# Joint conversion steps for the weight tiles, a ten-step inverse root and another written order at the start of a fused attention and feed-forward kernel

## The chip, the cores and the metric

One core of a Trainium2 chip runs the whole program. The metric is its device time in microseconds, from the first to the last instruction of an execution. Five engines work side by side, each through its own list of instructions in order: TensorE (PE, matrix products; its weight loads are PEld), VectorE (DVE), ScalarE (ACT), GpSimd (POOL) and SyncE (SP, which here issues the transfers). An instruction that waits for another engine or a transfer holds up everything behind it on its own engine.

## The reference

The program computes attention with a window of 32 and 32 global tokens, and then a gated feed-forward layer on the result:

```python
# 8 batches, 8 heads, 512 local and 32 global tokens, head size 64
out_g = np.matmul(sm(scale * q_g @ k_all.T), v_all)
s_ll = np.where(np.abs(pos[:, None] - pos[None, :]) <= 32, scale * q_l @ k_l.T, -1e9)
out_l = np.matmul(sm(np.concatenate([scale * q_l @ k_g.T, s_ll], -1)), v_all)
x = np.concatenate([out_g, out_l], 2)      # as 4608 tokens of 512
xn = x / np.sqrt(np.mean(x * x, -1) + 1e-6) * rms_g
g, val = xn @ w_gate, xn @ w_val           # 512 to 1536 each
y = (g / (1 + np.exp(-g)) * val) @ w_out   # 1536 to 512
```

The weights come as float64.

## The kernel before

The 4608 tokens are done in chunks. Chunk 0 is one batch of 512 local tokens. The attention of chunk 0 (units 0 to 3, each two heads) comes first, then its inverse root, its turned and scaled rows, and its feed-forward products, among which units 4 to 7 (the next chunk's attention) stand. All instructions of all engines stand in one list, ORDER, whose entries are chunk, step and piece, `0:g2.1` for the second piece of step g2 of chunk 0; each engine issues its own in that order. The steps are defined in JOBS's order, and in this order every tile draws its page of SBUF from the table PAGES (43 pages of 1024 words a partition, 8 wide ones) and its PSUM bank from BANKS. A transfer into a page can be issued only when the last reader of the page's former tile is done.

The letters of steps that the prediction speaks of, k being a number of a unit, a tile or a turn:
- L, V: loads of queries and keys, of values. S, M, E, T, C, A, X, Q, Z: scores (PE), mask (DVE), exponent (ACT), turn (PE), copy (ACT), value products (PE), division (DVE), squares (ACT), sums (DVE) of an attention unit.
- N0.i: the inverse root of chunk 0's mean squares, 13 small steps on DVE. D0: four diagonal 128x128 tiles with the roots (DVE). U0.k: PE turns the rows of x by multiplying with the diagonals, four 128x128 f32 matmuls for each k; H0.k (ACT) and Y0.k (DVE) write the high and low f16 halves.
- W: load of weight tile i, two transfers of 512 KB. Tiles 0 to 11 are the gate and value weights, 12 to 17 the output weights. m: rebias the exponent by a multiply (DVE if i is in MULT_V, else ACT). s: shift left by 3 (DVE). k or l: fetch the three low bits, on ACT ("three") if i is in LOW_A, else on DVE ("low"). g: put the sign in (DVE). q, p, e: squares and their scale (ACT, PE, DVE). a, d: high (ACT) and low (DVE) f16 weights.
- I f.wi: products of feed-forward tile f, six 128x512 f16 matmuls for each. B, b, h: its activation. O, o: output products and their end.

Each of m, k or l and g works on the two raw halves of a tile, one after another, 128x512 each; s, q, a and d work on 128x1024. All instructions go through one helper, so the trace names the one line L2095 for every row; tiles are told apart by kind (`page`, `bank`, `rn` for the root's small numbers, `ss` for the sums, `ws` for a weight scale, `wd` for a spilled tile in DRAM).

Of the kernel before, what the change touches and what calls it, by code (L numbers as in the profile page):

```python
# [2335 lines left out]
```

## Time and profile before

| | |
|---|---|
| median of 3 runs | 891.29 us (890.4 to 891.63) |
| profiled execution, span | 890.5 us |
| PE busy | 864.1 us, 97% |
| PEld busy | 666.4 us, 75% |
| DVE busy | 709.7 us, 80% |
| ACT busy | 557.9 us, 63% |
| POOL busy | 277.8 us, 31% |

A share is the busy time of an engine over the span. The span has very different stages, so the shares are read from the stage that a change touches.

### The profile page before, as it was taken

The numbers are of one execution on the slowest core, as the hardware profiler recorded it, in microseconds if no ns is written. First come the engines' busy times: TensorE is split into PE (matmuls) and PEld (weight loads), VectorE is DVE, ScalarE is ACT, GpSimd is POOL, SyncE is SP. The second block draws the span as 40 slices with busy tenths as digits, with TensorE's granted clock in tenths as the row PEclk, the third lists the DMA queues.
The fourth block names the chain that finished last, engine by engine and source line by source line (L and its number), as shares of the span: only waits on it lengthen the run. The fifth ranks groups of instructions, "written<-read, shape, count | busy, mean of one in ns | idle before, by whom it ended". The sixth has DMA issues, their size and how long they took to land.

```text
span 890.5 us, 28310 instructions
## 1 busy us (share of the span) xinstructions
PE 864.1 (97%) x11646; PEld 666.4 (75%) x11646; DVE 709.7 (80%) x1857; ACT 557.9 (63%) x1362; POOL 277.8 (31%) x255
## 2 busy tenths in 40 slices
PE   5599999999999999999999999999999999999998
PEld 4554455545548885588888888888888888888997
DVE  5999999798686776777886899688886798587576
ACT  6999993657344664557473876568575772545343
POOL 0000000024834475414531255123441344124414
PEclk9699999999999999999999999999999999999999
DMA  9995340488974997984697567968796759747671
GB/s 353 407 392 190 96 142 25 141 277 283 374 253 143 288 304 230 312 266 150 218 376 263 172 224 218 339 234 291 254 366 206 253 152 366 262 140 229 229 255 62
DMA packets 102737, 216.79 MB, mean 243 GB/s; under 512 B 8272, under 2 KB 34640, under 8 KB 102608
## 3 DMA queue, kind: packets, MB, share of 16 engines
q1 hardware_dynamic: 102176, 214.66, 70.9%
q8 instruction: 91, 1.49, 0.7%
q10 hardware_dynamic: 432, 0.33, 0.1%
q14 instruction: 38, 0.31, 0.1%
HBM read 187.96 MB, written 27.00 MB: 241 GB/s over the span
## 4 chain that ended last, share of the span: by engine, by line
PE 85%; DMA 3%; DVE 3%; issue 1%; ACT 1%; SPq 1%; POOL 0%; DVEq 0%; POOLq 0%; ACTq 0%
PE bank L2095 85%; DVE page L2095 3%; DMA wide<-wd 1%; DMA page<-in_vb_dram 1%; DMA page<-in_gv_dram 1%; ACT page L2095 1%; DMA wb<-page 1%; SPq L2095 1%; POOL page L2095 0%; DVE wide L2095 0%; DVE xg L2095 0%; DVE ws L2095 0%; DVE sm L2095 0%; DVE hs L2095 0%; DVE pow L2095 0%
## 5 line engine op out<-in xcount | busy, mean ns | idle before, releaser
L2095 PE MATMUL bank<-page,page 128*128 128x256 f16 (+7 forms) x8406 | 726.8, 277 | 16.4 <-ACT page L2095 8.0
L2095 PEld LDWEIGHTS <-page 128*128 128x128 f16 (+1 forms) x5568 | 515.7, 98 | 159.4 <-issue 7.6
L2095 POOL TENSOR_TENSOR page<-page,page 128x512 f16<-128x512 f32 (+5 forms) x163 | 180.0, 1122 | 286.4 <-ACT page L2095 236.1
L2095 DVE TENSOR_TENSOR page<-bank,page 128x512 f32<-128x512 f32 (+1 forms) x179 | 113.9, 649 | 64.2 <-PE bank L2095 37.5
L2095 ACT COPY page<-bank 128x512 f32<-128x512 f32 (+3 forms) x172 | 86.9, 529 | 111.2 <-PE bank L2095 100.0
L2095 ACT CAST page<-page 128x512 f16<-128x512 f32 (+2 forms) x144 | 109.0, 780 | 73.5 <-DVE page L2095 59.9
L2095 ACT ACTIVATE page<-page,sm 128x128 f32<-128x128 f32 x344 | 126.5, 391 | 26.7 <-DVE sm L2095 21.7
L2095 DVE TENSOR_TENSOR page<-page,page 128x256 f32<-128x256 f32 (+4 forms) x145 | 90.5, 636 | 9.0 <-ACT page L2095 7.0
L2095 POOL TENSOR_TENSOR page<-page,sm 128x512 f32<-128x512 f32 x22 | 25.5, 1167 | 208.9 <-DVE sm L2095 201.0
L2095 ACT ACTIVATE page<-page 128x512 f32<-128x512 f32 (+2 forms) x93 | 77.1, 907 | 9.6 <-DVE page L2095 7.2
L2095 DVE CUSTOM_DVE_ANT_0 page<-bank,page 128x128 f32<-128x128 f32 x248 | 60.3, 283 | 19.9 <-PE bank L2095 18.8
L2095 PEld LDWEIGHTS bank<-page,page 64*32 64x32 f32 (+4 forms) x3072 | 55.2, 113 | 24.5 <-issue 11.0
L2095 PE MATMUL bank<-wide,page 32*64 32x96 f32 (+6 forms) x2074 | 63.4, 266 | 1.3 <-DMA page<-in_vb_dram 1.3
L2095 ACT ACTIVATE page<-page,half_inv 128x512 f32<-128x512 f32 (+1 forms) x68 | 44.7, 686 | 23.9 <-DVE page L2095 19.3
L2095 DVE TENSOR_TENSOR page<-page 128x256 f32<-128x256 f32 (+3 forms) x110 | 57.1, 533 | 1.1 <-PE bank L2095 0.2
L2095 PE MATMUL bank<-page,wide 128*128 128x256 f16 (+4 forms) x500 | 56.9, 269 | 0.8 <-DMA wide<-wd 0.8
L2095 DVE SCALAR_TENSOR_TENSOR page<-page,page 128x512 f32<-128x512 f32 (+1 forms) x68 | 46.8, 702 | 12.7 <-ACT page L2095 12.7
L2095 DVE SCALAR_TENSOR_TENSOR page<-page,c_h,page 128x512 f32<-128x512 f32 (+1 forms) x73 | 51.8, 728 | 0.7
L2095 PEld LDWEIGHTS <-wide 128*128 128x128 f16 x450 | 41.6, 98 | 13.9 <-DMA wide<-wd 1.1
L2095 ACT ACTIVATION_READ_ACCUMULATOR page<-page,sm 128x1 f32 x248 | 46.8, 189 | 0.0
L2095 POOL TENSOR_TENSOR page<-wide,page 128x512 f16<-128x512 f32 (+2 forms) x25 | 27.4, 1105 | 45.4 <-ACT page L2095 43.3
L2095 PEld LDWEIGHTS bank<-wide,page 32*64 32x64 f32 (+2 forms) x1936 | 29.5, 129 | 6.8 <-issue 2.7
(156 smaller groups left out, 662.1 us busy)
## 6 DMA issues: line engine op xcount, KB each, us to landing
page<-wd SPq DMA_DIRECT2D x117, 512.0 KB, 6.9
page<-wb SPq DMA_DIRECT2D x36, 512.0 KB, 7.0
page<-in_w_in_dram SPq DMA_DIRECT2D x24, 512.0 KB, 9.3
page<-wa SPq DMA_DIRECT2D x23, 512.0 KB, 6.4
page<-wd SPq DMA_DIRECT2D x42, 256.0 KB, 5.3
page<-in_qkb_dram SPq DMA_DIRECT2D x23, 448.0 KB, 6.1
wide<-in_gkq_dram SPq DMA_DIRECT2D x16, 576.0 KB, 8.1
page<-in_vw_dram SPq DMA_DIRECT2D x16, 512.0 KB, 9.3
```

What stands on the lines that cost most here:

```text
L2095: return lambda *a, **k: write(self.engine, lambda: call(*a, **k))
```

## The change

1. CHAINS puts some pages side by side in one tile. Where the two raw halves of a weight tile lie on neighbouring pages, in either order, m, k or l and g run as one instruction over 1024 columns. That is so for all 18 tiles.
2. MULT_V and LOW_A change: seven tiles' multiply on DVE instead of six; tiles 3 and 14 have their low bits fetched on DVE, tile 15 on ACT.
3. The inverse root of chunks 0 and 1 takes ten steps: two rounds with other constants instead of three.
4. ORDER is written anew in its first part (636 entries before, 599 now), which is chunk 0 and the head of the next chunk. The 3118 entries behind it are the same.
5. PAGES (1198 entries) and BANKS (438) are new as a whole.

The code, with the tables ORDER, PAGES and BANKS left out:

```diff
@@ -38,85 +38,86 @@
...
-Q1 W3 X2 Q2 W4 W5 e0 Z1 a0 A3 X3 Q3 e1 a1 L7 Z2 Z3 N0.0 N0.1 N0.2 N0.3 N0.4 N0.5 m2 N0.6 N0.7 N0.8
-N0.9 N0.10 N0.11 N0.12 D0 U0.0 U0.1 U0.2 U0.3 k2 m3 k3 d0 s2 m4 s3 H0.0 H0.1 g2 s4 H0.2 H0.3 Y0.0
...
+W3 X2 Q2 W4 W5 e0 Z1 a0 A3 X3 Q3 e1 a1 L7 Z2 Z3 N0.0 N0.1 N0.2 N0.3 N0.4 N0.5 m2 N0.6 N0.7 N0.8 N0.9
+D0 U0.0 U0.1 U0.2 U0.3 k2 m3 k3 d0 s2 m4 s3 H0.0 H0.1 g2 s4 H0.2 H0.3 Y0.0 q2 Y0.1 Y0.2 L4 Y0.3 m5
...
 NPAGE, NWIDE = 43, 8
 
+CHAINS = (
+    (7, 8, 22, 25), (9, 10), (12, 11, 18), (13, 40), (14, 4, 27, 23, 39), (15, 26), (16, 17),
+    (28, 29), (30, 31), (32, 33), (34, 35), (41, 42),
+)
+
 ORDER = """
...
@@ -493,10 +494,19 @@
 
 
 
-    page = [con.tile([P, 1024], F32, tag=f"page{i}", name=f"page{i}") for i in range(NPAGE)]
+    page, link = {}, {}
+    for n, chain in enumerate(CHAINS):
+        whole = con.tile([P, 1024 * len(chain)], F32, tag=f"chain{n}", name=f"chain{n}")
+        for j, i in enumerate(chain):
+            page[i] = whole[:, 1024 * j : 1024 * (j + 1)]
+            if j:
+                link[chain[j - 1], i] = whole[:, 1024 * (j - 1) : 1024 * (j + 1)]
+    for i in range(NPAGE):
+        if i not in page:
+            page[i] = con.tile([P, 1024], F32, tag=f"page{i}", name=f"page{i}")
     wide = [con.tile([P, 1152], F32, tag=f"wide{i}", name=f"wide{i}") for i in range(NWIDE)]
     banks = [psum.tile([P, 512], F32, tag=f"bank{i}", name=f"bank{i}") for i in range(8)]
-    page_at, bank_at, smalls = iter(PAGES.split()), iter(BANKS.split()), [0]
+    page_at, bank_at, smalls, last_at = iter(PAGES.split()), iter(BANKS.split()), [0], [""]
 
     def tile_of(shape, dt, name):
         n = int(np.prod(shape[1:])) * (2 if dt in (F16, BF16) else 4) // 4
...
             return con.tile(shape, dt, tag=tag, name=tag)
-        at = next(page_at)
+        at = last_at[0] = next(page_at)
         if n > 1024:
             t = wide[int(at[1:])][:, :n]
         else:
@@ -575,12 +585,12 @@
             nc.gpsimd.tensor_tensor(dst, a, b, ALU.subtract)
 
 
-    MULT_V = (0, 1, 3, 7, 11, 12)
-    LOW_A = (2, 3, 4, 5, 6, 9, 10, 11, 13, 14, 16)
+    MULT_V = (0, 1, 3, 8, 9, 11, 15)
+    LOW_A = (2, 4, 5, 6, 9, 10, 11, 13, 15, 16)
     def raw_tile(name):
         return tile_of([P, 1024], I32, name)
 
-    job = {}
+    job, same_piece = {}, [False]
 
     def power(ps, n, top, dst):
 
...
@@ -646,15 +656,23 @@
     def convert(i):
 
         src = w_in[i] if i < NF else w_out[i - NF]
-        raws = []
+        raws, last = [], {}
         t = []
 
         def load():
+            pair, at = [], []
             for w in range(2):
-                raw = raw_tile(f"wr{i}{w}")
-                nc.sync.dma_start(raw, src[:, w, :].bitcast(I32))
-                r = raw.rearrange("p (n t) -> p n t", t=2)
-                raws.append((slice(w * 512, (w + 1) * 512), r[:, :, 0], r[:, :, 1], raw))
+                pair.append(raw_tile(f"wr{i}{w}"))
+                at.append(int(last_at[0][:-1]) if last_at[0][:1].isdigit() else -1)
+            turned = (at[1], at[0]) in link
+            for w in range(2):
+                nc.sync.dma_start(pair[w], src[:, 1 - w if turned else w, :].bitcast(I32))
+            both = link.get(tuple(at[::-1] if turned else at))
+            if both is not None:
+                raws.append((slice(0, 1024), both.bitcast(I32)))
+            else:
+                raws.extend((slice(w * 512, (w + 1) * 512), pair[w]) for w in range(2))
+            last[0] = pair[1]
 
         def rebias():
 
@@ -664,7 +682,9 @@
                 else raw_tile(f"w{i}t")
             )
             t32[i] = f32(t[0])
-            for c, _, hi, _ in raws:
+            for c, raw in raws:
+                hi = raw.rearrange("p (n t) -> p n t", t=2)[:, :, 1]
+                same_piece[0] = raw is not raws[0][1]
                 if i in MULT_V:
                     nc.vector.tensor_single_scalar(f32(t[0][:, c]), f32(hi), REBIAS, ALU.mult)
                 else:
@@ -675,14 +695,15 @@
 
         def three():
 
-            for _, _, _, raw in raws:
+            for _, raw in raws:
                 half = raw.bitcast(I16).rearrange("p (n t) -> p n t", t=4)
                 nc.scalar.activation(
                     half[:, :, 2], half[:, :, 1], AF.Copy, bias=-0.5 + 2.0**-14, scale=2.0**-13
                 )
 
         def low():
-            for _, _, _, raw in raws:
+            for _, raw in raws:
+                same_piece[0] = raw is not raws[0][1]
                 half = raw.bitcast(U16).rearrange("p (n t) -> p n t", t=4)
                 nc.vector.tensor_single_scalar(
                     half[:, :, 2], half[:, :, 1], 13, ALU.logical_shift_right
@@ -690,14 +711,16 @@
 
         def sign():
 
-            for c, _, hi, _ in raws:
+            for c, raw in raws:
+                same_piece[0] = raw is not raws[0][1]
+                hi = raw.rearrange("p (n t) -> p n t", t=2)[:, :, 1]
                 nc.vector.scalar_tensor_tensor(
                     t[0][:, c], hi, ends, t[0][:, c], ALU.bitwise_and, ALU.bitwise_or
                 )
 
         def squares():
             if i < NF:
-                sq_in[i] = raws[1][3].bitcast(BF16)[:, :1024]
+                sq_in[i] = last[0].bitcast(BF16)[:, :1024]
                 nc.scalar.activation(sq_in[i], t32[i], AF.Square, accum_out=ssq[:, i : i + 1])
             else:
                 junk = tile_of([P, 1024], BF16, f"wq{i}")
@@ -705,7 +728,7 @@
                     junk, t32[i], AF.Square, accum_out=rowsq[:, i - NF : i - NF + 1]
                 )
 
-        third = ("k", three) if i in LOW_A else ("l", low)
+        third = ("k", three if i in LOW_A else low)
         for n, fn in (("W", load), ("m", rebias), ("s", shift), third, ("g", sign), ("q", squares)):
             job[f"{n}{i}"] = fn
 
...
@@ -1306,13 +1329,26 @@
         steps = [
             lambda: nc.vector.tensor_reduce(z, ch["ss"], axis=AX.X, op=ALU.add),
             lambda: nc.vector.tensor_scalar(a, z, 1.0 / DM, 1.0e-6, ALU.mult, ALU.add),
-        ] + list(root_steps(a, y, z))
+        ] + list(root_short(a, y, z))
         for i, s in enumerate(steps):
             job[f"N{c}.{i}"] = s
         job[f"D{c}"] = factors
         for n, fn in zip("UHY", (turn, high, low)):
             for k in range(NK):
                 job[f"{n}{c}.{k}"] = lambda fn=fn, k=k: fn(k)
+
+    def root_short(a, y, z):
+        yi = y.bitcast(I32)
+        k = 0.375**0.5
+        yield lambda: nc.vector.tensor_scalar(
+            yi, a.bitcast(I32), -0.5, float(0x5F1FFFF9), ALU.mult, ALU.add
+        )
+        for first, second in ((-0.703952253, 0.703952253 * 2.38924456), (-k, 1.875)):
+            yield lambda: nc.vector.tensor_tensor(z, y, y, ALU.mult)
+            yield lambda w=first: nc.vector.scalar_tensor_tensor(z, z, w, a, ALU.mult, ALU.mult)
+            if second == 1.875:
+                yield lambda: nc.vector.scalar_tensor_tensor(z, z, 1.25 / k, z, ALU.add, ALU.mult)
+            yield lambda w=second: nc.vector.scalar_tensor_tensor(y, z, w, y, ALU.add, ALU.mult)
 
     def root_steps(a, y, z):
         yi = y.bitcast(I32)
@@ -2075,8 +2111,9 @@
 
     def write(engine, call):
         c, step, n, on = at_work
+        joined, same_piece[0] = same_piece[0], False
         if on and (on != engine or engine in ("vector", "gpsimd") or c and step[0] in "Rtn"):
-            n += 1
+            n += not (joined and on == engine)
         at_work[2:] = n, engine
         name = f"{c}:{step}.{n}"
         assert name not in plan or name == next(reversed(plan)), name

```

What the tables do to the order is shown at three places. First DVE, at the end of the inverse root and the diagonals of chunk 0 (`rn` holds the root, `ident` times `rn` is a diagonal, `ends` goes with the sign step). Before, with the sums' gathering on top:

```order
L2095 TENSOR_REDUCE rn_1_160<-ss_8_169 128x4
L2095 TENSOR_SCALAR rn_1_160<-rn_1_160 128x4 x3
L2095 TENSOR_TENSOR rn_1_160<-rn_1_160 128x4
L2095 SCALAR_TENSOR_TENSOR rn_1_160<-rn_1_160 128x4 x2
L2095 TENSOR_SCALAR page_71<-page_71 128x1024
L2095 TENSOR_TENSOR rn_1_160<-rn_1_160 128x4
L2095 SCALAR_TENSOR_TENSOR rn_1_160<-rn_1_160 128x4 x2
L2095 TENSOR_TENSOR rn_1_160<-rn_1_160 128x4
L2095 SCALAR_TENSOR_TENSOR rn_1_160<-rn_1_160 128x4 x2
L2095 SCALAR_TENSOR_TENSOR page_71<-page_74,ends,page_71 128x512
L2095 TENSOR_SCALAR page_95<-ident,rn_1_160 128x128 x4
L2095 SCALAR_TENSOR_TENSOR page_82<-page_70,ws_9_170,page_82 128x1024
```

After, from the seventh step of the root on:

```order
L2132 TENSOR_TENSOR rn_1_142<-rn_1_142 128x4
L2132 TENSOR_SCALAR hs<-bank_96,kk 128x1
L2132 SCALAR_TENSOR_TENSOR rn_1_142<-rn_1_142 128x4 x3
L2132 TENSOR_SCALAR page_82<-ident,rn_1_142 128x128 x2
L2132 TENSOR_SCALAR half_inv<-ws_11_154,ginv_e 128x1
L2132 TENSOR_SCALAR page_82<-ident,rn_1_142 128x128
L2132 TENSOR_SCALAR page_76<-page_76 128x1024
L2132 TENSOR_SCALAR page_82<-ident,rn_1_142 128x128
L2132 SCALAR_TENSOR_TENSOR page_76<-chain_63,ends,page_76 128x1024
L2132 SCALAR_TENSOR_TENSOR page_83<-chain_66,ws_9_152,page_83 128x1024
L2132 TENSOR_SCALAR page_77<-page_77 128x1024
```

The shift of tile 2 (128x1024) and its sign (now 128x1024 in one) have moved behind the root, the shift between the third and the fourth diagonal; two small scale steps (`hs`, `half_inv`) stand among the root's end and the diagonals.

Second PE, from the last value products of chunk 0 on (32x64) over the turns with the diagonals (128x128). Before:

```order
L2095 MATMUL bank_119<-page_84,page_76 32x64 x16
L2095 MATMUL bank_119<-page_77,page_76 32x64 x16
L2095 MATMUL bank_115<-page_95,page_80 128x128 x4
L2095 MATMUL bank_116<-page_95,page_87 128x128 x4
L2095 MATMUL bank_117<-page_95,page_87 128x128 x4
L2095 MATMUL bank_114<-page_95,page_80 128x128 x4
L2095 MATMUL bank_121<-page_69,page_95 32x128
L2095 MATMUL bank_120<-page_69,page_95 32x128
```

After, the same place, and then the end of the scale sum of tiles 2 and 3 with what follows it:

```order
L2132 MATMUL bank_101<-page_83,page_76 32x64 x16
L2132 MATMUL bank_96<-page_82,page_79 128x128 x4
L2132 MATMUL bank_98<-page_82,page_79 128x128 x4
L2132 MATMUL bank_101<-chain_67,chain_68 32x128
L2132 MATMUL bank_99<-chain_67,chain_68 32x128
L2132 MATMUL bank_103<-one_120,chain_64 128x1
L2132 MATMUL bank_96<-page_82,page_80 128x128 x4
L2132 MATMUL bank_100<-page_82,page_80 128x128 x4
L2132 LDWEIGHTS chain_65
L2132 MATMUL bank_102<-page_75,chain_65 128x512
```

Two of the four turns have moved behind the scores of unit 4 (32x128) and the scale sum (128x1). The first products (128x512) follow the fourth turn; before, they followed the scale sum.

Third DVE, the conversion of tile 1, the first to be converted. Before, the two halves from their two pages:

```order
L2095 TENSOR_SCALAR page_68<-page_70 128x512
L2095 TENSOR_REDUCE g_149<-gvec 128x1 x2
L2095 TENSOR_SCALAR page_70<-page_70 128x512
L2095 TENSOR_SCALAR page_68<-page_71 128x512
L2095 TENSOR_SCALAR page_68<-page_68 128x1024
L2095 TENSOR_SCALAR page_71<-page_71 128x512
L2095 SCALAR_TENSOR_TENSOR page_68<-page_70,ends,page_68 128x512
L2095 SCALAR_TENSOR_TENSOR page_68<-page_71,ends,page_68 128x512
```

After (ISA is the mask of a score tile and the reading of its minimum):

```order
L2132 TENSOR_SCALAR page_78<-chain_63 128x1024
L2132 TENSOR_SCALAR page_78<-page_78 128x1024
L2132 ISA page_75,sm_4_147<-bank_102,page_75 128x128
L2132 ISA sm_4_147 128x1
L2132 TENSOR_SCALAR chain_63<-chain_63 128x1024
L2132 ISA page_76,sm_4_147<-bank_103,page_75 128x128
L2132 ISA sm_4_147 128x1
L2132 SCALAR_TENSOR_TENSOR page_78<-chain_63,ends,page_78 128x1024
```

The halves have become one instruction each, and mask steps of the attention stand between them.

## Rows read from the trace of the kernel before

**Rows 1.** Windows: stretch, its us, busy us (x instructions) PE PEld DVE ACT POOL, PEclk, DMA share, GB/s

```profile
5.62:21.30 15.68, 13.17 (x344) 9.23 (x344) 11.65 (x80) 14.14 (x60) 0.00 (x0) 0.89 1.02 400
21.30:32.62 11.32, 8.86 (x227) 7.35 (x226) 10.21 (x33) 11.29 (x32) 0.00 (x0) 0.70 1.02 408
32.62:36.54 3.92, 0.00 (x1) 0.00 (x0) 3.59 (x12) 3.92 (x6) 0.00 (x0) 1.00 1.04 404
36.54:40.06 3.52, 0.00 (x0) 0.03 (x1) 3.31 (x15) 3.52 (x6) 0.00 (x0) 0.50 1.02 408
40.06:43.37 3.31, 3.31 (x15) 3.31 (x16) 3.31 (x5) 3.29 (x4) 0.00 (x0) 0.50 1.02 404
43.37:47.11 3.74, 3.74 (x102) 3.42 (x101) 3.74 (x9) 2.52 (x5) 0.00 (x0) 1.00 1.05 410
47.11:65.77 18.66, 17.43 (x117) 8.22 (x113) 18.05 (x55) 18.66 (x27) 0.00 (x0) 1.00 1.02 391
65.77:160.00 94.23, 94.23 (x908) 50.06 (x909) 90.74 (x216) 77.83 (x167) 0.00 (x0) 1.00 0.33 111
160.00:890.50 730.50, 723.40 (x9946) 584.80 (x9944) 564.71 (x1437) 422.76 (x1062) 277.60 (x251) 1.00 0.74 248
```

**Rows 2.** Timeline, PE: start, us, engine, line, op, out<-in, count [idle before <-releaser]

```profile
23.76 2.48 PE L2095 MATMUL bank<-ident,page 128*128 128x128 f32 x8 [2.46 <-ACT page L2095]
...
30.45 2.18 PE L2095 MATMUL bank<-page,page 128*32 128x64 f32 x128
40.06 6.47 PE L2095 MATMUL bank<-page,page 128*128 128x128 f32 x96 [7.44 <-ACT page L2095]
...
47.11 10.57 PE L2095 MATMUL bank<-page,page 128*128 128x512 f16 x48
...
61.36 0.38 PE L2095 MATMUL bank<-ssq,ones 128*128 128x2 f32 x2 [0.55 <-ACT page L2095]
...
65.77 0.45 PE L2095 MATMUL bank<-page,page 64*32 64x128 f32 x16 [0.68 <-DVE page L2095]
```

**Rows 3.** Timeline, DVE, from 9 to 48 us

```profile
9.96 0.29 DVE L2095 CUSTOM_DVE_ANT_0 page<-bank,page 128x128 f32<-128x128 f32 x1 [1.16 <-PE bank L2095]
...
30.32 0.16 DVE L2095 TENSOR_SCALAR pow<-bank 128x1 int32<-128x1 int32 x1 [0.96 <-PE bank L2095]
...
35.43 0.17 DVE L2095 TENSOR_REDUCE rn<-ss 128x4 f32<-128x16 f32 x1
...
36.72 0.68 DVE L2095 TENSOR_SCALAR page<-page 128x1024 int32<-128x1024 int32 x1
...
38.38 0.75 DVE L2095 SCALAR_TENSOR_TENSOR page<-page,ends,page 128x512 int32<-128x512 int32 x1
39.05 0.87 DVE L2095 TENSOR_SCALAR page<-ident,rn 128x128 f32<-128x128 f32 x4
```

**Rows 4.** Timeline, DVE, a tile's low, sign and low-half steps

```profile
52.55 1.32 DVE L2095 TENSOR_SCALAR page<-page 128x512 uint16<-128x512 uint16 x2
53.66 1.38 DVE L2095 SCALAR_TENSOR_TENSOR page<-page,ends,page 128x512 int32<-128x512 int32 x2
54.96 1.27 DVE L2095 SCALAR_TENSOR_TENSOR page<-page,ws,page 128x1024 f16<-128x1024 f32 x1
```

**Rows 5.** Lines by form, DVE, 0 to 200 us: busy us, mean ns | idle before

```profile
L2095 DVE TENSOR_SCALAR page<-page 128x512 f32<-128x512 f32 x10 | 4.2, 424 | 0.0
```

**Rows 6.** Timeline, ACT: a "three" step, a multiply and a whole-width pass

```profile
25.01 2.52 ACT L2095 ACTIVATE page<-page 128x512 int16<-128x512 int16 x2
...
57.94 1.29 ACT L2095 ACTIVATE page<-page 128x512 f32<-128x512 f32 x2
59.06 1.20 ACT L2095 ACTIVATE page<-page,ws 128x1024 f16<-128x1024 f32 x1
```

**Rows 7.** Timeline, PE, two late waits for transfers

```profile
309.52 1.48 PE L2095 MATMUL bank<-page,wide 128*128 128x256 f16 x12 [0.81 <-DMA wide<-wd]
...
433.65 2.35 PE L2095 MATMUL bank<-wide,page 32*64 32x256 f32 x158 [1.34 <-DMA page<-in_vb_dram]
```

More of the change, by code (lines that the diff above doesn't have):

```diff
@@ new lines @@
+m16 k16 M5.1 I11.00 m17 M5.0 C4.0 s16 I11.01 g16 q16 I11.10 I11.11 q14 k17 T4.1 C4.1 s15 E5.1 k15
+s17 T5.1 S7 g17 q12 q17 g15 q15 M7.1 A4 K0 K1 X4 E5.0 K2 S6 M6.0 a12 T5.0 d12 O0.0 O0.1 c8 Q4 r8 R5
+a13 d13 B11 b11 h11 O1.1 c9 c10 r10 a15 d15 O1.0 O0.3 O1.3 M7.0 C5.0 C5.1 c11 M6.1 O0.2 O1.2 a14 d14
+O2.0 O2.3 r9 O3.0 E7.0 A5 O2.2 E6.0 E6.1 J0 j0 Z4 O3.3 T6.0 R6 E7.1 u0 T6.1 r11 X5 a16 d16 Q5 Z5
+O3.2 V7 a17 d17 T7.1 V6 T7.0 R7 J2 C6.0 C6.1 A6 X6 O4.2 C7.0 C7.1 A7 X7 Q6 Z6 Q7 Z7 N1.0 O5.2 N1.1
@@ new lines @@
+0:M2.0.0 0:T0.0.0 0:C0.0.0 0:T0.1.0 0:z2.5 0:M2.0.2 0:E2.1.0 0:E2.0.0 0:S1.0 0:M1.1.0 0:T2.0.0
+0:M3.1.3 0:M3.1.2 0:E3.1.0 0:C0.1.0 0:M1.0.0 0:M3.0.0 0:T2.1.0 0:C2.0.0 0:C2.1.0 0:M1.1.1 0:W1.0
+0:m1.0 0:s1.0 0:M1.0.1 0:k1.0 0:M1.1.2 0:g1.0 0:M3.0.1 0:q1.0 0:p1.0 0:W3.0 0:m3.0 0:k3.0 0:M1.0.3
+0:M1.0.2 0:W0.0 0:m0.0 0:V0.0 0:A0.0 0:E3.0.0 0:z3.0 0:R2.0 0:T3.1.0 0:E1.0.0 0:T1.0.0 0:s3.0
+0:M1.1.3 0:E1.1.0 0:k0.0 0:s0.0 0:X0.0 0:Q0.0 0:z4.0 0:R3.0 0:g0.0 0:T1.1.0 0:C3.1.0 0:R1.0 0:C1.0.0
+0:C1.1.0 0:q0.0 0:e1.0 0:z4.1 0:z4.2 0:g3.0 0:V1.0 0:Z0.0 0:T3.0.0 0:e1.1 0:C3.0.0 0:q3.0 0:A1.0
@@ new lines @@
+0:X1.0 0:Q1.0 0:z5.0 0:z6.0 0:p0.0 0:e0.0 0:z6.1 0:z6.2 0:a1.0 0:V2.0 0:A2.0 0:X2.0 0:Z1.0 0:V3.0
+0:A3.0 0:e0.1 0:X3.0 0:e0.3 0:Q2.0 0:Z2.0 0:W2.0 0:Q3.0 0:Z3.0 0:e0.2 0:N0.0.0 0:N0.1.0 0:N0.2.0
+0:N0.3.0 0:N0.4.0 0:a0.0 0:e0.4 0:N0.5.0 0:N0.6.0 0:e1.3 0:N0.7.0 0:N0.8.0 0:m2.0 0:k2.0 0:W7.0
+0:m7.0 0:N0.9.0 0:D0.0 0:D0.1 0:e1.2 0:D0.2 0:s2.0 0:D0.3 0:U0.0.0 0:H0.0.0 0:g2.0 0:q2.0 0:d0.0
+0:U0.1.0 0:s7.0 0:L4.0 0:S4.0 0:Y0.0.0 0:M4.0.2 0:p2.0 0:e2.0 0:U0.2.0 0:U0.3.0 0:H0.1.0 0:d1.0
+0:Y0.1.0 0:I1.00.0 0:I0.10.0 0:W4.0 0:m4.0 0:k4.0 0:k7.0 0:e2.1 0:M4.1.0 0:e2.3 0:H0.2.0 0:s4.0
@@ new lines @@
+0:H0.3.0 0:Y0.2.0 0:I0.00.0 0:Y0.3.0 0:I0.01.0 0:L5.0 0:W5.0 0:m5.0 0:s5.0 0:M4.0.0 0:M4.0.3 0:g4.0
+0:I1.01.0 0:a2.0 0:d2.0 0:I1.10.0 0:I2.00.0 0:M4.1.3 0:I2.01.0 0:k5.0 0:g5.0 0:M4.1.1 0:B0.0
+0:M4.0.1 0:g7.0 0:I0.11.0 0:M4.1.2 0:L7.0 0:W8.0 0:a3.0 0:d3.0 0:e0.5 0:m8.0 0:b0.0 0:B1.0 0:b1.0
+0:q5.0 0:q4.0 0:p3.0 0:e3.0 0:E4.1.0 0:W11.0 0:S5.0 0:h0.0 0:M5.1.2 0:e3.3 0:W6.0 0:m6.0 0:M5.1.3
+0:s6.0 0:e1.4 0:k6.0 0:e3.1 0:a4.0 0:a5.0 0:I3.00.0 0:I3.10.0 0:W9.0 0:m9.0 0:e2.4 0:M5.0.2
+0:I3.01.0 0:k9.0 0:W10.0 0:e2.2 0:B2.0 0:B3.0 0:M5.1.1 0:g6.0 0:s9.0 0:q6.0 0:I1.11.0 0:d4.0 0:g9.0
@@ new lines @@
+0:I10.11.0 0:q16.0 0:q15.0 0:q17.0 0:c2.0 0:q14.0 0:d11.0 0:I11.10.0 0:T4.0.0 0:I11.11.0 0:B8.0
+0:B10.0 0:e6.5 0:C4.0.0 0:I11.00.0 0:g13.0 0:q13.0 0:K0.0 0:R4.0 0:k12.0 0:g12.0 0:b8.0 0:K0.1
+0:b10.0 0:I11.01.0 0:T4.1.0 0:r1.0 0:q12.0 0:K0.2 0:h8.0 0:K0.3 0:K1.0 0:h10.0 0:K2.0 0:K2.1
+0:M7.0.1 0:E5.0.0 0:T5.0.0 0:h9.0 0:K2.2 0:M7.0.3 0:c0.0 0:r0.0 0:C4.1.0 0:a12.0 0:d12.0 0:d12.1
+0:S6.0 0:M6.0.2 0:G.0 0:V4.0 0:A4.0 0:X4.0 0:c3.0 0:r3.0 0:C5.0.0 0:a13.0 0:d13.0 0:R5.0 0:r2.0
+0:T5.1.0 0:O0.2.0 0:M6.0.1 0:d13.1 0:K2.3 0:O0.1.0 0:a14.0 0:c4.0 0:r4.0 0:O0.3.0 0:O1.3.0 0:O1.2.0
@@ new lines @@
+0:O1.1.0 0:M6.0.0 0:d14.0 0:M6.0.3 0:B11.0 0:c5.0 0:M6.1.2 0:Q4.0 0:M6.1.1 0:O0.0.0 0:O1.0.0 0:a15.0
+0:d15.1 0:r5.0 0:M6.1.3 0:d14.1 0:b11.0 0:h11.0 0:d15.0 0:E7.0.0 0:E7.1.0 0:c10.0 0:c7.0 0:c6.0
+0:r6.0 0:C5.1.0 0:O2.2.0 0:r10.0 0:c9.0 0:M6.1.0 0:T7.0.0 1:w0.0 0:J2.0 0:a16.0 0:E6.0.0 0:r7.0
+0:O2.1.0 0:O2.0.0 0:T7.1.0 0:c8.0 0:C7.1.0 0:O2.3.0 0:C7.0.0 0:c11.0 0:r9.0 0:r8.0 1:w24.0 0:O3.0.0
+0:O3.1.0 0:E6.1.0 0:T6.1.0 0:a17.0 0:C6.1.0 0:T6.0.0 0:C6.0.0 1:w0.1 0:r11.0 0:R7.0 0:d16.0 0:R6.0
+1:w12.0 0:A7.0 0:X7.0 0:Q7.0 0:V5.0 0:A5.0 0:X5.0 0:d16.1 0:Q5.0 0:Z7.0 0:Z5.0 0:A6.0 0:O4.1.0
```

195 lines of the change are left out of this document (78 added, 117 removed), and 18 rows, old and new, of the table BANKS.

## The prediction

> **What bounds the kernel now.** I read the stretches first [rows 1], because one number over the whole span would hide the answer. From 65.77 us on TensorE (PE) is the bound: 94.23 of 94.23 us busy up to 160, then 723.40 of 730.50. Before 65.77 it isn't: it is busy 8.86 of 11.32 us, then not at all from 32.62 to 40.06, and 17.43 of 18.66 us at the end. The order differs only in the first 636 steps, the start with chunk 0 and the head of chunk 1, so the question is how much earlier PE becomes steadily busy and whether its feeders then keep up.
>
> PE's rows in order of time [rows 2] name the waits: 2.46 us before 23.76, 7.44 before 40.06, 0.55 before 61.36, 0.68 before 65.77. The row at 40.06 names ACT as the releaser, but DVE's rows [rows 3] show what it waited for: the sums of chunk 0 are gathered at 35.43, the inverse root runs in tiny instructions, its four diagonal tiles end at 39.05 + 0.87 = 39.92, and PE starts 0.14 us later. The granted clock in those stretches [rows 1] is 1.00 up to 36.54, 0.50 up to 43.37 and 1.00 after: PE idles from 32.63, the clock falls to 1.2 GHz, and the first 3.31 us of new matmuls run at that level.
>
> DVE is the feeder: 10.21 of 11.32, 3.59 of 3.92 and 18.05 of 18.66 us busy in the stretches from 21.30, 32.62 and 47.11. It has 15.68 - 11.65 = 4.0 us free between 5.62 and 21.30, 1.1 up to 32.62 and 3.5 between 65.77 and 160.
>
> **The change, part by part.**
>
> Joint steps. On DVE two half signs take 1.38 us, and a pass of the same kind over 1024 columns 1.27 [rows 4]: 0.11 saved a tile, 18 x 0.11 = 2.0 us. That the step reads every other word and the row shown doesn't is an unknown; bounds 0 and 0.15 a tile. DVE's 8 joint "low" steps and 7 joint multiplies I take at 0.1 each as the same saving, 1.5 us in all (bounds 0 and 2). On ACT two half multiplies take 1.29 us and a whole-width pass 1.20 [rows 6]: 0.09 for each of 11 multiplies and 10 "three" steps, 1.9 us.
>
> The Trainium skill, page "VectorE: DVE Perf Modes", section "The TRN2 errata", gives DVE's fixed cost per instruction as 58 cycles in its table and as about 150 cycles measured, at 0.96 GHz; by these the 18 joint signs would save an estimated 1.1 or 2.8 us. The rows' 0.11 stands between the two, and no term below goes by the page.
>
> Moved jobs. Tiles 3 and 14 go from ACT's "three" to DVE's "low", tile 15 the other way. On DVE that is one tile more at 1.32 us less 0.1; on ACT one tile less at 2.52 us [rows 4, 6]. The multiply list grows from six tiles to seven: 2 x 0.42 = 0.85 us more for DVE [rows 5]. All in all DVE: -2.0 - 1.5 + 1.2 + 0.85 = -1.4; two roots of three steps less, at 0.18 each (below), -1.1; together -2.5 us. ACT: -1.9 - 2.5 - 1.3 = -5.7 us. From 65.77 on this is hidden under PE and costs or gives nothing of itself; should PE have waited there it would be worth that much.
>
> Ahead of the root. Tile 3's "three" leaves ACT at 25.01, where the copies for PE's second value products stood behind its 2.52 us [rows 6], for DVE (+1.2). The joint steps of tiles 0, 1 and 3 ahead of the root give back 3 x 0.11 for signs and 5 x 0.1 for the rest, 0.8. With small scale steps that the order puts ahead, DVE's work to the root is 0.3 us more. Against it stand DVE's waits for PE, 1.16 us at 9.96 and 0.96 at 30.32 [rows 3], among the 5.1 free us: the new order puts conversions of tiles 1 and 3 where units of scores stood. I let it fill 1.3 (bounds: nothing, and 2.9), so the root starts 1.0 us earlier, at 34.4 (bounds 0.3 later, 2.6 earlier). The loads don't forbid it: the same tiles lie ahead of the last values, at the same 1.02 to 1.04 DMA share [rows 1].
>
> From the root to the first products, now 47.11 - 35.43 = 11.68 us [rows 2, 3]. Root steps: from 35.43 to 36.72 are seven, 0.184 each. Three fewer give 0.55; the shift of tile 2 between them (36.72 to 38.38 less six steps, 0.56) and the half sign of 0.67 ahead of the diagonals (38.38 to 39.05) go behind them. PE then starts after ten steps (1.84), two small ones (0.36), one diagonal (0.29, as the 128x128 pass at 9.96) and 0.14: 2.6 after the root instead of 4.63. But the products don't start 2.0 earlier for that. They need a low half that DVE now writes after this list: ten root steps and three small ones 2.4, diagonals 0.87, shift of tile 2 0.56, joint sign 1.27, two low-precision passes of tiles 0 and 1 2.54, a shift 0.56, one low half 0.75 (like the half sign at 38.38), a mask and two small ones 0.6, the second low half 0.6: 10.1 us, at 44.5. On PE the way is shorter: 2.6, two turn blocks 1.7 at the low clock (half of 3.31), the scores of unit 4 and a scale sum 3.74, two turn blocks at the full clock 0.9 [rows 1, 2]: 8.9. So DVE decides, the saving is 1.6, and with the 1.0 the first products start 2.6 us earlier.
>
> Behind it. DVE's next list, to the low weights of tile 2, ends by the same prices 7 us after that; PE wants them after six products, 6 x 1.3 = 7.8 (eight products are the 48 matmuls in 10.57 us at 47.11 [rows 2]). It fits with 0.8 to spare. Of the 1.23 us of waits at 61.36 and 65.77 the new order should remove half, 0.6: the sum that PE waited for at 61.36 is moved behind eight more products (bounds 0, 1.23). New small waits up to 160 I put at 0.5, since PE now asks 2.6 us sooner of a DVE with 3.5 us free (bounds 0, 3).
>
> New places. Every page and bank is drawn anew, also for the order's unchanged part. There PE waits 0.81 us at 309.52 for a fetch and 1.34 at 433.65 for values [rows 7]; fetches wait for a page to come free, so the places decide them. I take -0.5 (bounds: both gone, -2.15, and as much again, +2.15).
>
> Sum: -2.6 - 0.6 + 0.5 - 0.5 = -3.2 us. The profiled execution has 890.5 us, 0.8 below the median of 891.29 and inside the three runs; on the median the sum gives 888.1. About 0.2%, 1.8 us, is what a measurement can tell from no change.
>
> **The rivals.**
>
> The feeders don't follow (about 890.4). PE starts 2.6 us earlier, but the next weights come when they came before, and it waits in front of the second and third tile's products. For it: DVE's 18.05 of 18.66 us [rows 1] and the margin of 0.8. Against: DVE has 2.5 us less to do, ACT 5.7. It leaves 2.6 - 1.7 = 0.9 us.
>
> The clock comes back no earlier (about 889.3). If it is again 43.37 before the level is 1.00, the scores of unit 4 run their first 4.7 us at half speed, do 2.3 of the 3.74 us of work, and the products follow at 45.7: 1.4 gained instead of 2.6. For it: a gap is still there, about 32 to 37 us, and the row of before came back only after 3.31 us of work [rows 1]. The Trainium skill, page "TensorE: Matmul & The Clock Gate", section "What's actually happening", says that the default state is throttled and that activity releases it; by that rule an earlier start is followed by an earlier release, and the rival falls. The stretches agree with it as far as they go.
>
> Slower (about 893.5): the new places. Weights, values and spilled halves are fetched at a DMA share of 0.74 to the end [rows 1], and each fetch issues when its page's last reader is done. The gain of 3.2 less 0.5 for the places is 2.7; five new waits like the two shown, at 1.0 each, give 5.0, so the time is 2.3 longer. It decides from three such waits on (3 x 1.0 > 2.7). For it: all 1198 places are new, while the steps there kept their order. Against: only two waits of this kind stand in 730 us, so most pages have time to spare.
>
> That the joint steps don't happen would need the halves on unlinked pages; the order of after shows whole-width steps for every tile, so this is out. That a joint step over interleaved words costs as much as two halves takes 0.8 off the start and some 3.5 off DVE's saving; it belongs with the feeders.
>
> **How the numbers follow.** Forecast 0.55, feeders 0.20, clock 0.14, slower 0.11. Faster by over 0.2% means under 889.5: the forecast and about 0.6 of the clock case, 0.64. Within 0.2%: the feeders and the rest of the clock case, 0.25; slower 0.11. The time is the forecast's, 888.1. Low end: root 2.6 earlier, 1.6 behind it, 1.2 of waits: -5.4, 885.9. High end: past the feeders' case, 891.0; the slower case and the rest of the doubt stay outside.
>
> **What would show it.** Whole-width signs of tiles at 1.27 us on DVE, and no half ones; the root at 34.4 and PE's first turn block at 37.0; the first 512-column product at 44.5; no wait above 0.3 us between there and 75; PE's waits after 160 no longer than 7.1 in sum. The prediction is wrong if the root starts no earlier than 35.4, if PE waits for DVE or ACT again between 45 and 160 by more than 2 us, or if fetches behind 160 hold PE by more than before.

## The result, and the profile after

The changed kernel takes 900.69 us (median of four runs, 898.07 to 902.12), the kernel before 891.46 on the same chip: ratio 1.0097, 95% interval 1.0083 to 1.0111. It is 9.2 us slower where 3.2 faster was forecast. The page of after gives span and busy time:

```profile
span 900.3 us, 28280 instructions
...
PE 867.6 (96%) x11646; PEld 669.2 (74%) x11646; DVE 709.8 (79%) x1822; ACT 556.1 (62%) x1337; POOL 278.1 (31%) x255
```

DVE and ACT run 35 and 25 instructions less, yet DVE's busy time is the same as before. The stretches answer to [rows 1] (same columns):

```profile
38.46:40.00 1.54, 1.54 (x7) 1.54 (x8) 1.29 (x6) 1.54 (x2) 0.00 (x0) 0.51 1.04 404
40.00:42.09 2.09, 2.09 (x12) 1.97 (x11) 2.09 (x2) 2.09 (x3) 0.00 (x0) 0.54 1.03 406
42.09:45.69 3.60, 3.60 (x100) 3.39 (x100) 3.52 (x8) 3.57 (x5) 0.00 (x0) 1.00 1.03 400
...
38.46:65.00 26.54, 26.54 (x278) 16.50 (x279) 26.21 (x64) 26.33 (x33) 0.00 (x0) 0.94 1.02 390
65.00:160.00 95.00, 94.24 (x868) 50.24 (x866) 90.32 (x198) 78.08 (x153) 0.00 (x0) 1.00 0.31 116
...
237.50:246.00 8.50, 4.01 (x62) 2.07 (x69) 3.62 (x5) 1.31 (x2) 6.02 (x6) 0.64 1.04 363
311.00:320.00 9.00, 6.13 (x42) 4.86 (x41) 4.26 (x11) 5.42 (x16) 2.88 (x2) 0.81 1.05 374
160.00:900.30 740.30, 726.13 (x9934) 585.52 (x9932) 565.50 (x1435) 422.87 (x1060) 277.88 (x251) 0.99 0.72 245
```

The start is as forecast in kind: from 38.46 to 65 PE is never idle. The loss lies behind 160, where the same steps in the same order (but for the 2 us by which after is ahead there) take 740.30 us instead of 730.50 [rows 1]. PE is idle for 14.17 us of them, where the prediction's sign was no more than 7.1. In two places PE is busy 4.01 of 8.50 and 6.13 of 9.00 us at a lower clock. The window of before at the first of these places has PE at full load:

```profile
237.50:246.00 8.50, 8.46 (x159) 4.58 (x158) 6.14 (x24) 2.15 (x8) 7.23 (x7) 1.00 1.03 356
```

The timeline of after, by engine, at the start and at the two places (answering to [rows 2, 3]):

```profile
22.11 0.59 PE L2132 MATMUL bank<-ssq,ones 128*128 128x1 f32 x2 [4.68 <-ACT chain L2132]
...
38.46 3.70 PE L2132 MATMUL bank<-page,page 128*128 128x128 f32 x16 [4.87 <-DVE page L2132]
45.69 1.46 PE L2132 MATMUL bank<-page,chain 128*128 128x512 f16 x6
...
241.99 2.72 PE L2132 MATMUL bank<-page,page 128*128 128x512 f16 x6 [4.53 <-DVE chain L2132]
...
313.88 0.27 PE L2132 MATMUL bank<-chain,chain 128*128 128x256 f16 x1 [2.87 <-ACT chain L2132]
...
36.13 0.17 DVE L2132 TENSOR_REDUCE rn<-ss 128x4 f32<-128x16 f32 x1
...
37.53 0.55 DVE L2132 SCALAR_TENSOR_TENSOR rn<-rn 128x4 f32<-128x4 f32 x3
...
241.25 0.69 DVE L2132 SCALAR_TENSOR_TENSOR chain<-chain,bank 128x512 f32<-128x512 f32 x1 [7.06 <-ACT chain L2132]
...
240.53 0.69 ACT L2132 ACTIVATE chain<-bank,half_inv 128x512 f32<-128x512 f32 x1 [5.02 <-DMA wd<-chain]
...
312.64 0.72 ACT L2132 ACTIVATE chain<-page,half_inv 128x512 f32<-128x512 f32 x1 [3.56 <-DMA out_dram<-chain]
...
230.96 3.49 SPq L2132 DMA_DIRECT2D wd<-chain  x3
...
304.77 0.46 SPq L2132 DMA_DIRECT2D out_dram<-chain  x1
```

Read it from the end of the chain. PE waits 4.53 us for DVE, DVE had waited 7.06 for ACT, and ACT waited 5.02 for a *store* (`wd<-chain`, a transfer out of SBUF) before it could *write*. The tile it writes, the first of a feed-forward activation, has entry 263 of PAGES: page 13. The page's former tile is a converted weight tile whose spill to DRAM, the third of the three stores in SP's row, was issued at 233.73; ACT goes on at 240.53. Before, entry 263 was page 36; there the same step waits for no transfer:

```profile
237.22 0.67 ACT L2095 ACTIVATE page<-bank,half_inv 128x512 f32<-128x512 f32 x1
```

At 312.64 the same happens with entry 359 (page 41) behind the store of a block of the output issued at 304.77. Stores land late there. The DMA view of after from 230 to 240, at a DMA share of 1.09, gives KB each and median us from issue to landing:

```profile
wd<-chain SPq DMA_DIRECT2D x3, 256.0 KB, 7.9
wd<-chain SPq DMA_DIRECT2D x1, 512.0 KB, 6.7
```

From 174 to 181, at a share of 0.52, two such stores of 512 KB landed after 3.2 us:

```profile
wd<-chain SPq DMA_DIRECT2D x2, 512.0 KB, 3.2
```

The start of the same matmul in both kernels (after minus before, counted back from the last) gives the account:

```
after at   difference   what lies between
203.47       -1.97      the start: products 1.42 earlier, waits of 0.55 and 0.68 gone, 0.76 of new idle up to 160
241.99       +2.93      PE's wait of 4.53
246.35       +5.00      the low clock behind it
313.88       +7.95      PE's wait of 2.87
317.52       +9.19      the low clock behind it
317.94       +8.43      before's wait of 0.81 is gone
440.88       +7.24      before's wait of 1.34 is gone
448.85       +8.86      two new waits of 0.54 and 0.66
650.93       +9.55      small ones
end          +9.82
```

### The profile page after: what moved, and what is told of

Its sections match the earlier page's. It is cut to its first block, busy times and chain, and to the rows that moved or that the text cites. A ratio compares the mean times of both kernels' runs of the same rounds, so it can differ in the third digit from the quotient of the medians.

```text
span 900.3 us, 28280 instructions
## 1 busy us (share of the span) xinstructions
PE 867.6 (96%) x11646; PEld 669.2 (74%) x11646; DVE 709.8 (79%) x1822; ACT 556.1 (62%) x1337; POOL 278.1 (31%) x255
## 5 line engine op out<-in xcount | busy, mean ns | idle before, releaser
L2132 PEld LDWEIGHTS <-chain 128*128 128x128 f16 (+1 forms) x3744 | 346.3, 98 | 128.4 <-issue 12.9
L2132 PE MATMUL bank<-chain,chain 128*128 128x256 f16 (+6 forms) x3061 | 298.4, 270 | 5.0 <-ACT chain L2132 3.6
L2132 PE MATMUL bank<-page,chain 64*32 64x128 f32 (+5 forms) x1857 | 222.9, 298 | 1.2 <-ACT chain L2132 0.4
L2132 PEld LDWEIGHTS <-page 128*128 128x128 f16 x1704 | 160.7, 98 | 47.5 <-issue 7.8
L2132 POOL TENSOR_TENSOR chain<-chain,chain 128x512 f16<-128x512 f32 (+4 forms) x95 | 104.8, 1113 | 168.3 <-ACT chain L2132 128.3
L2132 PE MATMUL bank<-chain,page 128*128 128x256 f16 (+7 forms) x1377 | 151.8, 273 | 0.1
L2132 PE MATMUL bank<-page,page 64*32 64x128 f32 (+6 forms) x1231 | 105.0, 293 | 16.1 <-DMA page<-in_qk_dram 5.9
L2132 DVE TENSOR_TENSOR chain<-bank,chain 128x512 f32<-128x512 f32 (+1 forms) x106 | 67.4, 645 | 48.5 <-PE bank L2132 32.6
L2132 ACT ACTIVATE chain<-chain,sm 128x128 f32<-128x128 f32 x200 | 74.2, 391 | 23.4 <-DVE sm L2132 23.0
L2132 ACT ACTIVATE page<-page,sm 128x128 f32<-128x128 f32 x152 | 56.0, 391 | 4.4 <-DVE sm L2132 4.1
L2132 DVE CUSTOM_DVE_ANT_0 chain<-bank,wide 128x128 f32<-128x128 f32 x136 | 34.8, 283 | 12.5 <-PE bank L2132 10.1
```

The lines of the kernel that those rows point to most:

```text
L2132: return lambda *a, **k: write(self.engine, lambda: call(*a, **k))
```

## The experiments

Each ratio is to the kernel before on the same chip, with its 95% interval.

**Is it the places? Moving the two, and moving one into the old kernel.** In the first, two entries of after's PAGES move to pages from which no store is under way at that time:

```diff
@@ PAGES of after, entries 263 and 359
-13a
+16c
...
-41c
+24c
```

> The changed kernel with two entries of PAGES changed and nothing else: the tile that ACT writes at 240.53 us goes to page 16c in place of 13a, the one that it writes at 312.64 us to 24c in place of 41c; both new places are long empty. Theory 'places': these two writes wait for stores out of the page that they go to (5.02 and 3.56 us of ACT's time, 4.53 and 2.87 of PE's), and the low clock after each idle time adds some 2 and 1 us; both go, and the time falls by some 10 us to 890 (888.5 to 892). Rival 'transfers': the DMA engines are full in these stretches whatever the places, so the same wait turns up at the next fetch or store and the time falls by less than 4 us, to 896 or more. Rival 'joint steps': nothing changes, 900.

901.58 us, 1.0096 (1.0067 to 1.0124): nothing gained. The two waits are gone, but from the timeline another stands in their place:

```profile
249.71 0.61 PE L2133 MATMUL bank<-nt,same 128*128 128x16 f32 x2 [6.64 <-DVE sm L2133]
...
248.07 0.29 DVE L2133 CUSTOM_DVE_ANT_0 chain<-bank,wide 128x128 f32<-128x128 f32 x1 [6.03 <-DMA wd<-chain]
...
239.09 3.87 SPq L2133 DMA_DIRECT2D wd<-chain  x3
```

DVE's mask of a score tile, on another page, waits 6.03 us behind the next stores. In after the first held write had hidden most of this one: DVE came to the same mask only after its wait for ACT, when the store was nearly done:

```profile
248.68 0.29 DVE L2132 CUSTOM_DVE_ANT_0 chain<-bank,wide 128x128 f32<-128x128 f32 x1 [1.67 <-DMA wd<-chain]
```

A theory with two bad entries is too small.

The reverse puts one such place into the kernel before: entry 263 on a page from which a spill is under way.

```diff
@@ PAGES of before, entry 263
-36c
+8a
```

> The kernel before with one entry of PAGES changed: the tile that ACT writes at 237 us goes to 8a in place of 36c, onto a page whose store was issued some 3 us earlier, as in the changed kernel. Theory 'places': ACT waits 3 to 5 us for the store, PE behind it, and with the low clock after it the time rises by 5 to 7 us, to 897. Rivals: the place alone does nothing, 891.3.

894.56, 1.0023 (1.0012 to 1.0035): slower by some 2 us, not 5 to 7. ACT is held as in after, and PE for half as long:

```profile
241.74 0.69 ACT L2096 ACTIVATE page<-bank,half_inv 128x512 f32<-128x512 f32 x1 [4.43 <-DMA wd<-page]
...
243.20 3.04 PE L2096 MATMUL bank<-page,page 64*32 64x128 f32 x130 [2.36 <-DVE page L2096]
```

The sign of the mechanism is shown with one entry changed; the price expected was about three times the one measured. PE had other work until 240.84, 3.5 us past the 237.31 at which ACT was ready (in after only until 237.46, 2.0 past 235.51), and the clock stayed at 1.00 in the 5 us behind the wait. The rows show why PE had more work left. In both kernels PE waits for DVE's first step behind the held ACT write, which reads a PSUM bank. In after the product that waits is the first of a group of six; in this run PE still does these six and waits at the scores behind them. In before the two places lie 1.4 us apart. Neither matmul reads what that step writes, so PE presumably waits for the bank, and BANKS, new in after, would decide how soon PE needs it. That was not tested by itself.

**All places of the tail, both ways.** After with before's places for the tiles of the order's unchanged part (pages renamed; some 22 entries that would have collided with the new start chosen anew), and before with after's places there (some 17 chosen anew):

```diff
@@ PAGES of after, entries 185 to 1197: 975 differ; entry 263 and its neighbours
-8a 4a 13a 32a 41a W7a
+42a 36a 37c 12a 16a 35a
@@ PAGES of before, entries 185 to 1197: 980 differ; entry 263 and its neighbours
-34a 2a 36c 10a 13a 41a
+8a 37a 35a 36a 38a 6a
```

> The changed kernel with new places for the tiles of the order's unchanged part: those of the kernel before, with page numbers renamed to fit round the tiles that the first part leaves (some 20 tiles that don't fit stand elsewhere); the first part and the banks stay. Theory 'places': the whole loss behind 230 us goes and the 2 us of the start stay: 889.4 (888 to 891.5), with waits near those of before at 309 and 433. Rival 'transfers': the earlier start makes the fetches collide, 895 or more. Rival 'joint steps': 898 or more.

> The kernel before, its order, joint steps none, its first part with its own places; the tiles of the unchanged part of the order get the places of the changed kernel, renamed to fit (some 17 that don't fit stand elsewhere). Theory 'places': it loses what the changed kernel loses behind 230 us, 6 to 11 us, to 898 to 903, by waits for stores at about 238 to 250 and at 310. Rival 'transfers' (the earlier start is what makes stores and writes meet): 892 to 894.

| | before's places in the tail | after's places in the tail |
|---|---|---|
| order, steps, root, banks of before | 1 | 1.0165 (1.015 to 1.0179), 907.12 us |
| order, steps, root, banks of after | 0.9969 (0.9955 to 0.9983), 889.96 us; again: 0.998 (0.9969 to 0.9991), 890.7 | 1.0097 (1.0083 to 1.0111) |

> The second experiment again, in more rounds, beside the kernel with halves and long root: a ratio of 0.996 to 0.998 as before.

Places alone cost 15 us without any new step, more than the 6 to 11 expected; everything else alone makes the kernel 1.6 and 2.7 us faster in the two measurements. So neither the joint steps nor the earlier start are needed for the loss. In the waits (us in total, times, longest) of the before kernel with the new places, behind 160, transfers out hold both ACT and DVE:

```profile
ACT page L2096 <- DMA wd<-page: 7.7, 1, 7.7
...
DVE page L2096 <- DMA wd<-page: 5.4, 3, 4.2
...
ACT page L2096 <- DMA out_dram<-page: 3.3, 1, 3.3
```

and of after with before's places there is one such row, with PE's own waits at most 1.3:

```profile
PE bank L2133 <- issue: 1.3, 1, 1.3
ACT chain L2133 <- DMA out_dram<-chain: 0.8, 2, 0.4
PE bank L2133 <- DMA chain<-in_vb_dram: 0.6, 1, 0.6
```

**How many places does it take?** Sixteen entries of after moved, and then six:

```diff
@@ PAGES of after, sixteen entries: 203 241 250 263 284 286 287 289 302 359 368 406 415 426 432 1151
-27a 3c 17a 13a 10a 25a 39a 39a 25c 41c 8a 29a 29a 29c 14c 24a
+35a 17a W7a 7a W5a 16c 7a 25c W2a 16c 24c 23a 23c W7a W3d W0a
@@ PAGES of after, six entries: 263 286 287 302 359 368
-13a 25a 39a 25c 41c 8a
+16c W2a W2c 16c 24c 36c
```

> The changed kernel with 16 entries of PAGES changed: nearly every tile that ACT, DVE or GpSimd first writes less than some 12 us after a store out of its page was issued goes to a page that is long empty (the two of the first experiment among them). Theory 'places, in a chain': the writes behind stores stand one after another, and the first wait hides the next ones, so that all have to go: 890 to 892, with no wait of PE above 1.5 us behind 230. Rival 'transfers': the full DMA engines hold PE elsewhere, at fetches that come late: 895 or more.

> The changed kernel with six entries of PAGES changed: the two of the first experiment and four tiles that DVE first writes between 248 and 304 us, each to a place whose former store or reader is over 4 us done and whose next fetch is over 10 us away, so that no fetch is held in SP's queue as in the run with sixteen places. Theory 'places, on both sides of a tile': 889.5 to 892, no wait of PE above 1.5 us behind 230. If a wait of 2 us or more stands there again, it must lead back to a store or to a fetch held by a page's reader; else the theory falls.

895.41, 1.0042 (1.0028 to 1.0057), and 895.70, 1.0044 (1.0028 to 1.006), where 890 to 892 was expected: each takes back a little over half of the loss, not all. With sixteen, entry 250 now lies on a wide page and holds a *fetch* (`wide<-in_qkb`) in SP's queue until 229.96, for a reader of that page on GpSimd, and every store behind it comes later. PE waits 3.71 at 243.60 for DVE, DVE waited 5.49 for GpSimd, and GpSimd had stood idle for 5.80 with no cause in the records; that the late transfers are the cause isn't shown. With six, DVE's write to the page of another spilled tile is held, and PE waits 2.53 for DVE at 266.65. Between the two DVE is never idle for more than 0.9 us, so the delay seems carried along its list:

```profile
250.45 1.23 DVE L2133 TENSOR_TENSOR chain<-chain 128x1024 f32<-128x1024 f16 x1 [4.98 <-DMA wd<-chain]
```

So the places are bad as a set: moving two, six or sixteen leaves or uncovers other waits.

**What the joint steps, the root and the order are worth.** Halves again instead of joint steps, in after (the pages and the order kept), and in after with before's places; 13 root steps instead of ten; and both:

```diff
-            if j:
-                link[chain[j - 1], i] = whole[:, 1024 * (j - 1) : 1024 * (j + 1)]
...
-        ] + list(root_short(a, y, z))
+        ] + list(root_steps(a, y, z))
```

> The changed kernel without joint steps: every m, k or l and g runs as two halves of 512 columns again, at the place in the order where the joint one stood; order, pages and banks are those of the changed kernel. Theory 'places': the tail keeps its two waits; the start gets later by what the joint steps gave, 0 to 1 us: 900 to 902. Rival 'joint steps': whole-width steps over two pages are what costs, and the time falls below 896.

> The kernel of the second experiment (changed first part, old places behind it) without joint steps: halves again at the same place in the order. By the predicted prices the joint steps give DVE 0.8 us ahead of the root and 3.5 us in all, so without them the first products stand 0.8 us later or more, 890.8 to 892. If a joint step costs as much as its two halves, as the rows of the changed kernel say for the low step (1.31 against 1.32 us), no more than 0.5 us: 890 to 890.5.

> The kernel of the second experiment with the inverse root of 13 steps in place of ten for chunks 0 and 1, the three more steps right behind the ten. By the predicted price, three steps at 0.18 us on the path to the diagonals: 0.55 us later, 890.5. If PE's start is set by something else than DVE's list, no change, 890.0.

> The kernel of the second experiment with halves and with the inverse root of 13 steps: of the changed first part only the order, its own places and the moved jobs are left. If the three parts add up as measured one by one (0.2% for joint steps, 0.3% for the root), the gain of the second experiment is gone: 892, a ratio of 1.001. If the new order alone carries it: 890.5, a ratio of 0.998.

Halves in after: 899.86, 1.0073 (1.0058 to 1.0088), with the same two waits (4.40 and 2.41), so the joint steps are not what makes the loss. Whether they have a small part in it, 1.0073 against after's 1.0097, is not told apart: the intervals still meet, and behind the wait of 2.41 the clock stayed at 1.00. With before's places:

| | ten root steps | 13 root steps |
|---|---|---|
| joint | 0.9969 and 0.998 (as above) | 0.9996 (0.9987 to 1.0004), 891.62 us |
| halves | 0.9988 (0.9978 to 0.9998), 890.69 us | 1.0 (0.9987 to 1.0013), 892.01 us |

By the medians the root is worth 0.1 to 0.3% and the joint steps 0 to 0.2%, and order and moved jobs with neither gain nothing. Of the root's pairs two have intervals that overlap, so no more than its sign is likely, and of the joint steps not even that. The long root with joint steps was expected at 890.5 and came at 891.62. On PE the three more steps show as 0.59 us of wait ahead of the turns, first with ten and then with 13. The first products come only 0.29 us later for them, at 46.79 and not 46.50, which is 0.03% of the time:

```profile
38.44 3.81 PE L2133 MATMUL bank<-page,page 128*128 128x128 f32 x16 [4.87 <-DVE page L2133]
```

```profile
39.02 3.81 PE L2133 MATMUL bank<-page,page 128*128 128x128 f32 x16 [5.46 <-DVE page L2133]
```

## Why the prediction was wrong

**The step that failed** is "New places ... I take -0.5 (bounds: both gone, -2.15, and as much again, +2.15)". The two waits did go, -2.15. In their place came +7.0 (4.53 of wait and some 2.4 of low clock or small change behind it), +4.2 (2.87 and some 1.3), +1.6 and about 1.2 of small ones: +11.8 net. The bound was drawn from the waits that before shows, fetches behind a page's last reader [rows 7]. What came is the mirror image, an engine's write behind a store that still reads the page. It was within reach, for the waits of before behind 160 hold a few such rows, this the longest, and both tables could have been laid beside the stores:

```profile
ACT page L2095 <- DMA out_dram<-page: 2.2, 1, 2.2
```

Exchanging the tables alone, but for the some 20 entries that did not fit, shows that the places are the cause (1.0165 one way, 0.9969 the other).

**The rival "slower: the new places"** named the right part, with the wrong wait and price: not five fetches at 1.0 but two held writes at 4 to 7 each, clock included. That is why it ended at 893.5 and not at 900.

**Ahead of the root: "1.0 us earlier, at 34.4".** Wrong: 36.13, 0.7 later, past its bound of 0.3. It is no matter of one execution: in the six with this start the root stands at 35.81 to 36.56, in the three with before's start at 35.35 to 35.81. A likely part is PE's wait for ACT at 22.11, 4.68 us where it was 2.46 [rows 2]: the new order asks ACT for a tile's squares there before the value products. That it delays the root wasn't tested.

**From the root to the first products: 10.1.** Measured 9.56 (45.69 less 36.13), and to the first turns 2.33 where 2.6 was said. The root steps' 0.55 measured 0.59. But "DVE decides" was wrong. PE waits for nothing between its first turn and the first product, so PE's own way sets the time, and its 8.9 came from a misread row. The four turn blocks of before are 32 matmuls:

```profile
L2095 PE MATMUL bank<-page,page 128*128 128x128 f32 x32 | 5.4, 346 | 7.4 <-ACT page L2095 7.4
```

The 3.31 us at the low clock hold 15 of them [rows 1], two blocks and not four, and the other two are in the 3.74 us behind. In after two blocks took 3.63 us (1.7 said), scores and scale sum 1.73 (3.74 said, with two blocks in it), the last two blocks 1.87 (0.9 said). The saving is 2.1 where 1.6 was said, and with the root 0.7 late the products came 1.4 earlier, not 2.6.

**Behind it.** Both waits of before are gone (1.23; 0.6 said), and PE's new idle time from 65 to 160 is 95.00 - 94.24 = 0.76 (0.5 said). The start is -1.97 against -2.6 - 0.6 + 0.5 = -2.7: near, partly because errors cancel. With before's places it shows in the time as 0.2 to 0.3%.

**The joint steps.** The view by line and shape of after, up to 200 us (count | busy us, mean ns):

```profile
L2132 ACT ACTIVATE chain<-chain 128x1024 int16<-128x1024 int16 x10 | 24.8, 2507 | 0.1
L2132 DVE TENSOR_SCALAR chain<-chain 128x1024 uint16<-128x1024 uint16 x8 | 10.5, 1310 | 0.0
L2132 DVE SCALAR_TENSOR_TENSOR chain<-chain,ends,chain 128x1024 int32<-128x1024 int32 x8 | 10.2, 1274 | 1.1 <-ACT chain L2132 1.0
L2132 ACT ACTIVATE chain<-chain 128x1024 f32<-128x1024 f32 x5 | 6.0, 1194 | 0.0
```

A sign takes 1.27 to 1.28 against 1.38 for two halves [rows 4]: the 0.1 that was forecast, 1.8 us for 18. By the two fixed costs that the Trainium skill, page "VectorE: DVE Perf Modes", section "The TRN2 errata", gives, an estimate for the 18 is 1.1 or 2.8 us. The trace stays between. The 16-bit steps save nothing: "low" 1.31 against 1.32 [rows 4], "three" 2.51 against 2.52 [rows 6]. So DVE's -2.5 and ACT's -5.7 us were too much; the page's totals are 709.8 (709.7 before) and 556.1 (557.9). It cost nothing, since PE hides them.

**The rivals about the start.** The feeders follow: PE is busy 26.54 of 26.54 us from 38.46 on (the 1.7 us that this rival takes off its 2.6 stands in no row). The clock comes back earlier in this execution: 0.51 and 0.54 in the stretches up to 42.09 and 1.00 from there, so near 41.9 instead of 43.37. But not in every execution with this start. In the second experiment, after with before's places, PE's work begins at 38.44, the level stays low until 43.84, and the products come at 46.50 and not near 45.7:

```profile
38.44:43.84 5.40, 5.40 (x80) 5.03 (x80) 5.00 (x9) 5.40 (x7) 0.00 (x0) 0.50 1.04 403
46.50 1.46 PE L2133 MATMUL bank<-page,chain 128*128 128x512 f16 x6
```

The same kernel measured again had them at 46.24. So the rival "the clock comes back no earlier" holds in that execution, and takes 0.8 us of the start's gain there; its own 45.7 equals after's 45.69 by chance, since after's delay is the root's. The prediction let this rival fall by the rule of the Trainium skill, page "TensorE: Matmul & The Clock Gate", section "What's actually happening", that activity releases the clock. After agrees with what it drew from the rule, an earlier start and so an earlier release; the second experiment does not (start 1.6 us earlier, release 0.5 later than before), and the measurement decides.

**Left open.** What keeps the versions with six and sixteen moved places 5 us above the one with all of before's is shown only as far as their largest waits. Why before with after's places loses more (15 us) than after itself isn't shown, nor what BANKS adds to a held write. The share of the joint steps is within the spread. A wait of PE of 0.4 to 1.8 us with no cause in the records ("issue") near 640 to 650 stands in the versions with the new start; before has 0.1 there, before with one bad place 0.4, and before with the new places 0.5 at 657. It was not followed up.

## What to carry to other kernels

A page has two kinds of last reader. If the last is a store, the next writer waits for the store's landing, which here came 6.7 to 7.9 us after its issue where the DMA share was 1.09. When places are drawn anew, look for each store at who writes the page next and how soon, on the engines in order, and judge the table as a whole: a held write gives the stores time and so hides the next one. Here the tables lost 11.8 us where the start had gained 2; test order and places apart, by exchanging the tables.

## What the runs showed of the hardware

A pause of PE cost more than itself, but not always. The granted clock over the 5 us behind each pause of over 2 us in the tail, by windows:

| PE's pause, us | clock behind it |
|---|---|
| 2.36 (before, one bad place), 2.36 (before, new places), 2.41 (after, halves) | 1.00, 1.00, 1.00 |
| 2.53 (after, six places), 2.59 (before, new places), 2.87 (after) | 0.66, 0.66, 0.67 |
| 3.71 (after, sixteen places), 4.40 (after, halves), 4.53 (after) | 0.69, 0.50, 0.53 |
| 5.62 (before, new places), 6.64 (after, two places) | 0.55, 0.65 |

At 0.5 to 0.7 of full speed over 5 us the engine loses another 1.5 to 2.5 us (an estimate from the table), so of pauses a few tenths apart one cost nearly 2 us more than the other. The length alone does not tell: at the start of before, with other pauses near it, the 2.46 us ahead of 23.76 have 0.50 behind them. And a joined step over 16-bit words of interleaved data saved 0.01 us on DVE (1.31 against 1.32) and on ACT (2.51 against 2.52), where the joined 32-bit sign saved 0.1.
